# Rows of v by SP transfers split by parity on the DRAM side, and a new order of all steps, in a fused long-convolution and MLP-mixer kernel

## The chip, the cores and the metric

The kernel runs on one core of a Trainium2 chip. The metric is the device time of one execution in microseconds (us). A core has TensorE (PE), VectorE (DVE), ScalarE (ACT), GpSimd (POOL) and SyncE (SP, which only issues transfers), each with an instruction stream of its own that runs in order, and 16 DMA engines that move data between the DRAM and the on-chip memory (SBUF, 128 partitions). PE writes its sums to PSUM, from where DVE and ACT take them.

## The reference

Two blocks work on the same x = A_q (2048 rows of 640 numbers, bfloat16) and a gate mixes them. The inputs A_k and A_v have the same shape; B_x is not used.

```python
k_shift = sum over t in 0..3 of k shifted down by 3-t rows, times shift_k[:, 3-t]   # short causal convolution
kv = k_shift * v
y  = irfft(rfft(kv, 4096) * rfft(ssm_k, 4096))[:2048] + kv * ssm_D      # long causal convolution
a  = q * y
h  = gelu(layernorm(x) @ w1)            # w1 640 x 640
hs = (four groups of 160 columns of h, shifted by +1, -1, +2, -2 rows) @ w2
x1 = x + hs
b  = x1 + gelu(layernorm(x1) @ w3) @ w4     # w3 640 x 1536, w4 1536 x 640
g  = sigmoid((x * gate_w).sum(-1))
out = g * a + (1 - g) * b
```

## The kernel before

Partition p holds the 16 rows 16p to 16p+15 of x, k and v; a "tile" t1 (0 to 15) is one such row of every partition, and four tiles make a chunk c. A transfer of one chunk moves, for each of the 128 partitions, 4 × 640 numbers that lie side by side in DRAM (5120 B), 640 KB in all. The row views `q_rows`, `k_rows`, `v_rows` (L63) have this form.

**v and its rows.** The transform of kv works on even and odd p apart, so the tile KV (R1) holds v with even p in partitions 0 to 63 and odd p in 64 to 127. `v_load(c)` (L571) fills chunk c through `take` (L172): an indirect transfer, issued by POOL (L174), which takes for each partition the DRAM row named in ROWS. `row_order` (L218) writes ROWS by two iota instructions. Four such gathers load v.

**kv.** `k_load(c)` brings k (L560) and transposes it on PE with the same parity (KT). `tap(q)` works on one half of the tiles (q // 5: 1 is tiles 8 to 15, which need v2 and v3; 0 is tiles 0 to 7, with v0 and v1) and one group of 128 columns (q % 5): PE makes the four-tap convolution of k by small matmuls (L590); then either ACT copies it out of PSUM (L598) and DVE multiplies it into KV in place (L601), or DVE multiplies from PSUM (L604).

**Long convolution.** A transform in steps: `step1` on PE (KV at L424, the kernels of ssm_k at L422, loaded by `load_h`, L187), copies out of PSUM by ACT (L369) or DVE (L371), a round trip through DRAM (S_x, S_h; sent at L434, gathered at L441), `step2` (L462), `product` (DVE), `step3` (L509, sent at L520 to S_g), `gin` (L534, back from S_g), and `step4` (PE L875), whose result is multiplied by q and the gate, by ACT (L879) and DVE (L882) or by DVE alone (L885), and added to the sum in X. Its q comes by `load_q(c)` (L858), a transfer on SP, one for each chunk.

**MLP.** `load_x` (L190, L193), `x_stats(c)` (row statistics: DVE bn_stats L684 or two ACT passes with a row sum, L678 and L680), `x_norm` (L661, L663), `x_turn` (transposed by PE, or by a transfer, L651), `mlp1(c, u)` (W1, loaded at L196; PE L709, gelu on ACT L712; its sums lie in the two PSUM banks `psm`), row shifts, `w2` (weights L206 and L207: the first transfer brings four groups of 128 rows, the second the last 32 rows of each group, 4 × 32 rows onto 128 partitions; PE L786), `x1_norm`, `w3` (PE L834, gelu L839), `w4` (PE L852, DVE L854), `store` (L845). Small single-row transfers are ssm_D's (L405) and Zs (L728).

**Order.** `ORDER` (L893 on) is one list for the whole kernel, such as `v_load.3:0`: the step name, its arguments and which piece of it. Each engine runs its instructions in the order in which this list emits them; nothing reorders them later. Letters in a name say which engine evicts (A for ACT, V for DVE). `SLOTS` (L66) says for each allocation of a tag which of its buffers it takes: tag c is four PSUM banks, m the two psm banks, row, gt, xt, gq, ax, hp are SBUF rings. An allocation waits until the users before it in that buffer are done.

SP issues nearly all transfers, in one queue, and its first ones are, in order: x0 (two halves), k3, k1, k2, shift_k, x1, k0, W1, x3, W2 (two), x2, h3, h0, gate_w. POOL issues v3, v2, v0, v1 beside them.

Of the kernel before, what the change touches and what calls it, by code (L numbers as in the profile page):

```python
# [16 lines left out]
P = 128  # L17
S = 2048
D = 640
F = 1536  # L20
NT = 16
# [20 lines left out]
def kernel(  # L42
# [17 lines left out]
    V, A, G, PE, SP = nc.vector, nc.scalar, nc.gpsimd, nc.tensor, nc.sync  # L60
# [6 lines left out]
        "c": "012310320123102130120132013021320321010231302301203120321302103120302130213023012301203102310230"  # L67
             "123013201230312312010132013013012031023302131203012213020132030210312031023301230213102321003212"
             "130120310230132103210232031130220313120132002132013201323100231103232010123302130213021302130132"
             "0012301230123013213",  # L70
        "m": "01010101010101010101010101010101010101010101010101010101010101010101",
        "row": "01230132013120023102130213012030213030301",
        "gt": "012312002103120123012301201",
        "xt": "010101",
        "gq": "01210212012021012012101210110120120",
        "ax": "0123021302310312",
        "hp": "01231302",
# [91 lines left out]
    def by_row():  # L169
        return bass.IndirectOffsetOnAxis(ap=ROWS[:], axis=0)  # L170

    def take(dst, rows, t):  # L172

        G.indirect_dma_start(out=dst, out_offset=None, in_=rows, in_offset=by_row(), element_offset=t * D)  # L174
# [686 lines left out]
    def step4(t1, ev):  # L861
# [240 lines left out]
```

## Time and profile before

| | us |
|---|---|
| median of 3 runs (238.97 to 239.47) | 239.30 |
| the profiled execution | 239.24 |
| its span, first to last instruction | 237.5 |
| PE busy | 224.6 |
| DVE busy | 194.7 |
| ACT busy | 174.0 |
| POOL busy | 16.9 |

The profile tells of one execution. The span is shorter than the execution by what lies before the first and after the last instruction. Busy time of an engine is the sum of its instructions; a row such as `PE 8986...` gives the busy share, in tenths, in each of 40 equal slices of the span (some 5.9 us each). In the lists of instructions a row has the start, the busy time, the engine, the line of the kernel, the operation, what is written and read, and how many of them stand in the row; in brackets, how long the engine was idle before it and what released it. For a transfer the trace also keeps landing records: one time stamp for each DMA engine whose share has landed, up to 16 for a transfer (some records are missing). v's four gathers landed at 17.72 to 19.85 (v3), 19.82 to 21.98 (v2), 28.67 to 30.11 (v0) and 30.33 to 32.70 us (v1); x2 landed at 23.62 to 26.94.

### The profile page before, as it was taken

What the parts mean: (1) busy time and instruction counts of PE and PEld (TensorE: products, weight loads), DVE (VectorE), ACT (ScalarE), POOL (GpSimd) and SP (SyncE); (2) the same over time, 40 slices, a digit from 0 to 9 for tenths busy, and PEclk for the clock granted to TensorE, in tenths of its full rate; (3) what the DMA queues carried; (4) which work ended last, traced back from release to release, by engine and by line L of the source; (5) the groups of instructions that cost most, each with busy time, mean ns of one, the idle gap of its engine ahead of it and who ended that gap; (6) DMA issues with size and microseconds to landing.
All of it is one profiled execution on the core that took longest, in us unless ns stands there. A gap on an engine that the chain in (4) does not pass through costs nothing.

```text
span 237.5 us, 5627 instructions
## 1 busy us (share of the span) xinstructions
PE 224.6 (95%) x2241; PEld 115.8 (49%) x2260; DVE 194.7 (82%) x458; ACT 174.0 (73%) x311; POOL 16.9 (7%) x34
## 2 busy tenths in 40 slices
PE   8986999999999999999999999999999999999791
PEld 3764655533755555444544343444444445456551
DVE  7996999998998999875798897686895988129793
ACT  4796999878887989999697887673698533547560
POOL 4415022000000200021200000000000000000000
PEclk9999999999999999999999999999999999999999
DMA  6999919761999699996899902499950456399672
GB/s 248 375 391 353 359 60 197 182 246 56 382 354 294 212 361 208 353 385 261 286 278 190 354 1 89 130 272 317 360 163 5 139 196 198 138 272 369 190 276 110
DMA packets 42743, 57.06 MB, mean 240 GB/s; under 512 B 20313, under 2 KB 35418, under 8 KB 42462
## 3 DMA queue, kind: packets, MB, share of 16 engines
q1 hardware_dynamic: 42142, 54.10, 71.3%
q0 software_dynamic: 576, 2.62, 2.8%
q8 instruction: 17, 0.28, 0.5%
q14 instruction: 8, 0.07, 0.1%
HBM read 34.42 MB, written 18.36 MB: 222 GB/s over the span
## 4 chain that ended last, share of the span: by engine, by line
PE 87%; DMA 5%; DVE 3%; issue 2%; ACT 1%; SPq 0%; ACTq 0%
PE ps L834 22%; PE ps L852 20%; PE psm L709 10%; PE psw L786 9%; PE ps L462 5%; DMA WA<-in_B_w_dram 5%; PE ps L875 4%; PE ps L422 4%; PE psk L590 3%; PE ps L509 3%; PE psz L227 3%; PE ps L424 3%; PE pst L395 2%; PE pst L618 1%; DVE X L854 1%
## 5 line engine op out<-in xcount | busy, mean ns | idle before, releaser
L852 PE MATMUL ps<-W,gt 128*128 128x128 bf16 (+1 forms) x370 | 54.7, 296 | 1.2 <-issue 0.8
L834 PE MATMUL ps<-x1t,W 128*128 128x512 bf16 x240 | 55.6, 380 | 0.0
L852 PEld LDWEIGHTS <-gt 128*128 128x128 bf16 x384 | 29.0, 98 | 25.2 <-issue 4.9
L834 PEld LDWEIGHTS <-W 128*128 128x128 bf16 x240 | 21.9, 98 | 28.5 <-issue 4.7
L369 ACT CAST gs<-ps 128x320 bf16<-128x320 f32 x40 | 14.9, 433 | 20.4 <-PE ps L509 14.0
L369 ACT CAST stg<-ps 128x512 bf16<-128x512 f32 x46 | 24.8, 594 | 6.7 <-PE ps L424 3.7
L839 ACT ACTIVATE gt<-ps 128x1024 bf16<-128x1024 f32 x24 | 24.7, 1036 | 3.9 <-PE ps L834 3.8
L709 PE MATMUL psm<-xt,WA 128*128 128x512 bf16 x100 | 23.5, 380 | 1.8 <-DMA WA<-in_B_w_dram 1.8
L371 DVE CAST stg<-ps 128x512 bf16<-128x512 f32 x34 | 22.5, 684 | 2.1 <-PE ps L422 1.3
L786 PE MATMUL psw<-WA,HT 128*128 128x128 bf16 (+1 forms) x112 | 21.1, 296 | 0.4 <-issue 0.2
L879 ACT ACTIVATE y<-ps,GS 128x320 bf16<-128x320 f32 x23 | 11.5, 527 | 8.7 <-PE ps L875 6.4
L369 ACT CAST hs<-ps 128x512 bf16<-128x512 f32 x25 | 13.6, 598 | 3.4 <-PE ps L462 3.4
L371 DVE CAST XS<-ps 128x512 bf16<-128x512 f32 x17 | 11.3, 685 | 5.6 <-PE ps L462 5.6
L369 ACT CAST XS<-ps 128x512 bf16<-128x512 f32 x23 | 12.6, 595 | 4.2 <-PE ps L462 4.1
L709 PEld LDWEIGHTS <-WA 128*128 128x128 bf16 x100 | 9.0, 98 | 13.3 <-DMA WA<-in_B_w_dram 2.0
L371 DVE CAST hs<-ps 128x512 bf16<-128x512 f32 x15 | 10.1, 688 | 6.6 <-PE ps L462 6.5
L371 DVE CAST gs<-ps 128x320 bf16<-128x320 f32 x24 | 11.1, 486 | 5.2 <-PE ps L509 4.7
L786 PEld LDWEIGHTS <-HT 128*128 128x128 bf16 x116 | 10.0, 98 | 10.5 <-issue 0.8
L854 DVE SCALAR_TENSOR_TENSOR X<-ps,OMG,X 128x640 bf16<-128x640 f32 x16 | 14.0, 877 | 0.6 <-PE ps L852 0.6
L462 PE MATMUL ps<-ax,CMP 64*32 64x512 bf16 (+3 forms) x512 | 12.9, 300 | 0.1
L885 DVE SCALAR_TENSOR_TENSOR q<-ps,GS,q 128x320 bf16<-128x320 f32 x9 | 4.8, 546 | 10.0 <-PE ps L875 10.0
L788 DVE SCALAR_TENSOR_TENSOR X<-psw,X 128x640 bf16<-128x640 f32 x16 | 12.9, 818 | 0.2
(150 smaller groups left out, 362.6 us busy)
## 6 DMA issues: line engine op xcount, KB each, us to landing
S_x<-stg SPq DMA_DIRECT2D x8, 640.0 KB
S_h<-stg SPq DMA_DIRECT2D x8, 640.0 KB
ax<-S_x SPq DMA_DIRECT2D x8, 640.0 KB
ax<-S_h SPq DMA_DIRECT2D x8, 640.0 KB
S_g<-gs SPq DMA_DIRECT2D x8, 640.0 KB
W<-in_B_w_dram SPq DMA_DIRECT2D x2, 1920.0 KB
kn<-in_A_k_dram SPq DMA_DIRECT2D x4, 640.0 KB
q<-in_A_q_dram SPq DMA_DIRECT2D x4, 640.0 KB
```

Of the source, the lines that this page charges most:

```text
L369: A.copy(out=dst, in_=src)
L371: V.tensor_copy(out=dst, in_=src)
L422: PE.matmul(ps[r][:], lhsT=F1N[:, r].rearrange("p a b -> p (a b)"), rhs=src[:, o + 512 * u:o + 512 * u + 512], start=True, stop=True)
L462: PE.matmul(ps[j][q:q + 32, lo - 512 * u:hi - 512 * u], lhsT=CMP[HALF[j], 8 * b + 4 * h + i, c, :], rhs=st[name, 2 * b + h][HALF[j], i, lo ...
L709: PE.matmul(ps[:, v, :].rearrange("p (a b) -> p a b", a=4), lhsT=W1N[:, k, 160 * f:160 * f + P] if f < 4 else W1M[:, k, :], rhs=xt[:, :, k ...
L786: PE.matmul(ps[:, o:o + w], lhsT=h_tile(f, t1), rhs=W2P[:, f, o:o + w], start=(f == 0), stop=(f == 4))
L788: V.scalar_tensor_tensor(out=X1[:, t1, :], in0=ps[:], scalar=1.0, in1=X[:, t1, :], op0=ALU.mult, op1=ALU.add, accum_out=S12[:, 0, t1:t1 + 1])
L834: PE.matmul(ps[:, u, :].rearrange("p (a b) -> p a b", a=4), lhsT=st["W3"][:, k, f * P:(f + 1) * P], rhs=xt[:, :, k, :], start=(k == 0), st ...
L839: A.activation(out=gt[:, 2 * (fp % 2):2 * (fp % 2) + 2, :], in_=ps[:], func=ACT.Gelu_apprx_tanh)
L852: PE.matmul(ps[:, o:o + w], lhsT=st["gt", c, f // 4][:, f % 4, i * P:(i + 1) * P], rhs=st["W4"][:, f, o:o + w], start=(f == 0), stop=(f == ...
L854: V.scalar_tensor_tensor(out=X1[:, t1, :], in0=ps[:], scalar=OMG[:, t1:t1 + 1], in1=X1[:, t1, :], op0=ALU.mult, op1=ALU.add)
L879: A.activation(out=box["y"][:], in_=box["ps"][:], func=ACT.Copy, scale=GS[:, t1:t1 + 1])
```

## The change

`take` no longer gathers by indices on POOL. It issues on SP a plain transfer whose DRAM side is written out by hand: two groups (even p, odd p), 64 rows in each, 4 × 640 numbers in a row. The SBUF side is the 128 partitions as before. The bytes and the size of a packet stay.

```diff
 def take(dst, rows, t):
-    G.indirect_dma_start(out=dst, out_offset=None, in_=rows, in_offset=by_row(), element_offset=t * D)
+    SP.dma_start(out=dst, in_=bass.AP(tensor=rows.tensor, offset=rows.offset + t * D, ap=[[NT * D, 2], [2 * NT * D, P // 2], [1, 4 * D]]))
```

In the built program the DRAM side has the outer sizes 2, 64 and the SBUF side 128.

`ORDER` is written anew from beginning to end, and with it the strings of `SLOTS` for c, row, gt, gq, ax and hp and some of the letters that choose the evicting engine. The parts that the prediction speaks of:

```diff
-        "open.L1.left:0 open.A2.right:0 warm:0 load_x0.0:0 consts0:0 warm:1 kv_alloc:0 pow0:0 warm:2 load_x0.1:0 "
-        "consts0:1 f1_table:0 k_load.3.AAA:0 row_order:0 f1n_table:0 x_stats.0.VVVA:0 k_load.1.VAA:0 warm:3 f1n_table:1 "
...
+        "k_load.0.AVV:0 k_load.1.AAA:1 x_stats.0.VVVA:5 k_load.3.AAA:4 load_w1:0 v_load.3:0 k_load.1.AAA:4 kv_consts:0 "
+        "k_load.2.AAV:1 k_load.1.AAA:2 x_stats.0.VVVA:6 k_load.1.AAA:6 k_load.2.AAV:3 x_norm.0.VVVV:0 v_load.2:0 "
+        "x_norm.0.VVVV:1 x_norm.0.VVVV:2 k_load.2.AAV:5 k_load.2.AAV:2 k_load.2.AAV:4 x_norm.0.VVVV:3 load_x.3:0 "
+        "k_load.2.AAV:6 x_turn.0.VAV:0 x_turn.0.VAV:1 x_turn.0.VAV:4 v_load.0:0 x_turn.0.VAV:2 x_turn.0.VAV:3 "
+        "x_turn.0.VAV:5 v_load.1:0 f1n_table:1 x_stats.1.VVVV:0 tap.7.AA:0 tap.7.AA:1 tap.9.VA:0 load_h.2:0 tap.7.AA:3 "
...
+        "tap.6.VA:0 tap.6.VA:1 load_x.2:0 tap.5.AV:2 load_w2:0 x_stats.3.VVAA:1 k_load.0.AVV:3 tap.8.VA:3 "
...
+        "x_norm.3.VVVV:3 mlp1.1.1:0 tap.3.AA:1 tap.4.AV:4 x_turn.3.D:0 step1.KV.3.VAAAAVAAAA:0 x_stats.2.VVAA:0 "
```

SP's first transfers are then, in order: x0 (two halves), k3, k1, shift_k, k2, x1, k0, W1, v3, v2, x3, v0, v1, h2, x2, W2 (two), gate_w, h1, h3. `row_order` stands late, where nothing uses what it writes. At the end of the kernel `load_q.1` and `load_q.2` stand just before `gin.0.1` and `gin.0.2`; before, `load_q.2` stood behind `gin.1.1`, after six more gin transfers, and `load_q.1` well ahead of the first gin. ACT loads its function tables five times where it did so six times. PE's 2260 matmuls are the same, and from the middle of the long convolution on nearly in the same order.

More of the change, by code (lines that the diff above doesn't have):

```diff
@@ L66 @@
     SLOTS = {
[L67 to L70, printed above, removed]
+        "c": "012310230212312031231201320132013023131201032120312032013031203120310213201320310123120321031023"
+             "120301230120321031223132013201203210123301230212301012313201302132032103102132032103102132020131"
+             "320123030210312312013202301201331023210231032103102103201233210102321033210213003123012301231203"
+             "1023102301203210212",
         "m": "01010101010101010101010101010101010101010101010101010101010101010101",
-        "row": "01230132013120023102130213012030213030301",
-        "gt": "012312002103120123012301201",
+        "row": "01230120312103032130210231320132021021021",
+        "gt": "012301212312323012301201301",
         "xt": "010101",
-        "gq": "01210212012021012012101210110120120",
-        "ax": "0123021302310312",
-        "hp": "01231302",
+        "gq": "01220221012120120121012021021201201",
+        "ax": "0123031203210312",
+        "hp": "01230312",
     }
```

297 rows, old and new, of the table ORDER are left out of this document.

## The prediction

> **What bounds the kernel now.** I read the page's busy shares first, then its 40 slices, then the table of waits, then the windows and the timeline of 10 to 45 us and of the end.
>
> ```profile
> span 237.5 us, 5627 instructions
> PE 224.6 (95%) x2241; PEld 115.8 (49%) x2260; DVE 194.7 (82%) x458; ACT 174.0 (73%) x311; POOL 16.9 (7%) x34
> PE   8986999999999999999999999999999999999791
> POOL 4415022000000200021200000000000000000000
> DMA  6999919761999699996899902499950456399672
> ```
>
> TensorE is busy 224.6 of 237.5 us; only the start and the last three slices have room. POOL, whose queue issues the four gathers of v, is busy 7%: it is no bound, and freeing it buys nothing by itself. The DMA row shows 9s at the start: there the 16 DMA engines are full.
>
> ```profile
> PE psm L709 <- DMA WA<-in_B_w_dram: 1.8, 1, 1.8
> DVE KV L604 <- DMA KV<-in_A_v_dram,ROWS: 1.8, 1, 1.8
> PE ps L875 <- DVE q L885: 1.2, 1, 1.2
> ```
>
> The columns are total us, times, longest. PE waits 1.8 us for W1 at 20.05, DVE 1.8 us for v at 22.08, and PE 1.2 us at 221.61 for DVE L885, which itself waited until 221.01 for the q rows of `load_q.2` (landed 218.55 to 220.92).
>
> ```profile
> 15.00:20.00 5.00, 3.16 (x56) 2.53 (x54) 4.83 (x20) 4.98 (x10) 0.30 (x1) 1.00 1.02 398
> 30.00:35.00 5.00, 5.00 (x60) 2.85 (x60) 4.63 (x18) 5.00 (x11) 1.34 (x2) 1.00 0.17 55
> 35.00:40.00 5.00, 5.00 (x60) 2.82 (x61) 4.86 (x17) 4.88 (x11) 0.76 (x1) 1.00 0.94 130
> ```
>
> Columns: window, length, busy us of PE, PEld, DVE, ACT, POOL (instructions), granted clock, DMA share, GB/s. In 15 to 20 us DMA is full and ACT and DVE are saturated, so an earlier W1 alone could give little. From 30 us on PE has no gap, and it has none up to the end stage: **whatever delays PE at 40 us delays the end one for one.**
>
> **Parts of the change, one: how many engines carry a load of v.** A gather of v (640 KB, 128 packets of 5120 B) landed in 1.4 to 2.4 us by its landing records (one for each engine's share: v3 17.72 to 19.85, v0 28.67 to 30.11, 16 records each). The new transfer moves the same 128 packets, but its DRAM side begins with an outer size of 2 and its SBUF side with 128. What does the trace show of transfers whose sides begin with different sizes? Those that begin with 128 (or gin's 64 against 32) leave up to 16 records. The second W2 transfer (L207), which begins with 4 on the DRAM side and 128 on the SBUF side, leaves three (24.58 to 25.63), while L206 beside it leaves 15. The single-row transfers (ssm_D L405, Zs L728) leave two each: one about 0.16 us after the issue ends and before data could be there (L728: 55.28), one when the data has landed (56.01). So a transfer need not use all 16 engines, and the missing shares are reported at once. It is not proof: x1's 128-row load left 7 records, so records get lost. I read it as: the number of engines is what divides both outer sizes, at most 16. For v that is **2 engines**, 64 packets each; the other end is 16.
>
> The Trainium skill, page "DMA: Bandwidth & Descriptors", section "Why a DMA increments its semaphore by 16 and not by 1", states this rule: the largest k up to 16 that divides the slowest dimension (other than 1) of both patterns, and on queues such as SP's the lowest-numbered k engines. By it all four loads go through the same pair of engines. The records of L207 and L728 agree as far as they go; no run here shows which engines they were.
>
> Price: a 5120 B packet takes 196 ns (median of this size; mean 219 with the crowded start). 64 × 0.196 = 12.5 us for a load, against 8 × 0.196 = 1.6 on 16 engines; the k loads, each 1.6 to 2 us behind the last, agree with that.
>
> **Two: the queue behind them.** SP's order is new: x0, x0, k3, k1, shift_k, k2, x1, k0, W1, v3, v2, x3, v0, v1, h2, x2, W2 (two), gw, h1, h3. Each engine serves its shares in this order (landings of one queue follow the issue order in the trace). The pair is free when its share of W1 is done: before, 14 of W1's 16 records fell at 14.91 to 15.41, the last at 20.00 behind gathers; I take 16.0 (15.0 to 17.4). Then
> - v3 at 28.5, v2 at 41.1;
> - x3's share, 8 × 0.196 = 1.6: 42.7;
> - v0 at 55.2, v1 at 67.7;
> - h2's share, 8 packets of 4096 B by 159 ns, 1.3: 69.0;
> - x2's share, 1.6: **70.6**.
>
> The gathers had landed by 32.70, x2 by 26.94.
>
> **Three: who waits.** DVE needs v2 and v3 for taps 5 to 9 and v0 and v1 for taps 0 to 4. It now stops at its first v3 product until 41 and works some 12 us of taps and x3 statistics up to 53. The next, tap 4's product (L604), waits for v1 until 67.7; behind it in DVE's order stand all its statistics of x2, later taps and evictions. ACT stands at its first pass over x2 (L678), and behind that, in its order, are the gelus of `mlp1` chunk 1 (L712) that free the two psm banks; PE stands at `mlp1.1.2` for that bank. All three engines are in order, so nothing overtakes. The rows:
>
> ```profile
> 32.42 0.76 ACT L678 ACTIVATE jk<-X 128x640 bf16<-128x640 bf16 x1
> 32.83 0.69 DVE L604 TENSOR_TENSOR KV<-psk,KV 128x512 bf16<-128x512 f32 x1 [0.27 <-PE psk L590]
> 37.97 1.94 ACT L712 ACTIVATE HT<-psm 128x1024 bf16<-128x1024 f32 x2
> 39.60 1.25 PE L709 MATMUL psm<-xt,WA 128*128 128x512 bf16 x5
> ```
>
> ACT's first x2 pass goes from 32.42 to 70.6, 38.2 us later. PE had the bank at about 39.0 and came to it at 39.60, so 0.6 is slack: **+37.6** on PE. By DVE's way (32.83 to 67.7) it is 34.9, so x2 decides. If ACT does the casts that stood between these rows (2.75 us: L598 1.58, L369 0.59 and 0.58) during its wait, the shift is 34.9 instead; its order has them behind the x2 pass, so I take 37.6.
> The transfers behind x2 (W2, h1, h3) land 2 to 4 us later than it; their users stand at 50 us and more in the old order, some 88 in the new, so they are covered. S_x sends and the h loads come later still.
>
> **Four: PE's clock after a stop.** PE will stand for some 25 us. The first 11 warm-up matmuls come 0.425 us apart, later ones 0.216, though the granted clock reads 1.00 throughout. At most this start is paid again (11 × 0.21 = 2.3), at least nothing; **+1.0**, since behind the stop PE waits on ACT and DVE in places.
>
> **Five: the end.** `load_q.2` (issued at 212.53 behind six gin loads) now comes before `gin.0.1` and `gin.0.2`. The 1.2 us of PE's wait and DVE's go: −1.3. `gin.0.2`, issued at 207.08 and landed at 211.25 with its user at 211.80, comes behind two more transfers: +0.7 (0 to 2). ACT loads its function tables 5 times instead of 6; the one at 130.07 (1.28 us, begun while ACT waited 1.26 for PE): −0.3 (−1.3 to 0). Together **−0.9**.
> The gathers gone from POOL (4 × 1.0 us) and `row_order` moved late: 0, POOL is idle beside them. DVE and ACT exchange some evictions, PE's 2260 matmuls are the same and from 90 us on almost in the same order: 0 (−1 to +1), since PE stays the bound there.
>
> **Sum.** Against the profiled execution, 239.24 us (span 237.5; the median of the runs is 239.30, so nothing is lost between them): 239.24 + 37.6 + 1.0 − 0.9 = 276.9, so **277 us**. Low: start 15.0 (−1.0), no casts in between (−2.7), no cold clock (−1.0), end −1.5 more: 270.7. High: start 17.4 (+1.4), packets at their mean of 219 ns (256 of them on the pair's way, +6), cold +1.3: 285.6. So 270 to 286.
>
> **Rivals.**
> - *All 16 engines carry v* (L207's records are merely lost). Then v lands 1.6 us a piece from about 17 on, without POOL's issues between; W1 is no longer held to 20.00 by gathers. The waits at 20.05 and 22.08 go, but ACT's 4.98 of 5 us in 15 to 20 leaves some 0.5 of it. 239.24 − 0.5 − 0.9 = **237.8** (236 to 238.7), faster. Against it: the early landing records of L728.
> - *Sixteen engines, and the new order costs more than it gives*: `gin.0.2` behind q.2 and `gin.0.1`, 1 MB or 2.6 us of all engines, comes to its user 2 us late, of which 1.3 is not won back, and x2 behind both v0 and v1 is 0.3 late: **240.3**, slower. It decides when `gin.0.2` lands later than 211.8 plus the shift.
> - *Two engines, but another pair for each load*: the four run side by side, each 12.5 us from about 16 on, v3 by 28.5, v0 and v1 by 31 to 33. DVE's first product moves from 22.08 to 28.5, 6.4 us, and x2 is not held. 239.24 + 6.4 − 0.9 = **244.7** (243 to 248). Nothing in the trace tells which engines a transfer takes.
> - *No measurable change*: what the start gives, `gin.0.2` takes.
>
> **Chances.** Same pair (270 to 286) 0.80; sixteen and faster 0.08; own pairs 0.06; sixteen and slower 0.04; no change 0.02. A measurement of this kernel tells about 0.2% (0.5 us) from no change. The forecast's own range holds 8 in 10 by itself. Faster 0.08, same 0.02, slower 0.90.
>
> **What would show it.** In the profile after, v's four loads should land 12 to 13 us behind each other (28, 41, 55, 68), two records each beside the early one; the 40 slices should show PE, DVE and ACT near 0 between about 24 and 70 us and a DMA share near 2/16; the table of waits should name KV <- DMA v for DVE (some 15 + 15 us) and x2 for ACT; PE's wait for L885 at the end should be gone. If v lands within 2 us of its issue, step one is wrong and the first rival holds; if the four land together near 30, the third.

## The result, and the profile after

The changed kernel takes **286.86 us** (285.53 to 288.84), the kernel before 239.24 us (238.97 to 239.47): ratio 1.1998, 95% interval 1.1926 to 1.207. The forecast was 277, 270 to 286: the direction and the two long stops came as predicted, but the time is 10 us above the forecast and just above its range. The profiled execution took 287.11 us.

First the page of the changed kernel, the lines that answer to those of before.

```profile
span 285.3 us, 5618 instructions
PE 232.0 (81%) x2241; PEld 117.8 (41%) x2260; DVE 193.4 (68%) x456; ACT 174.0 (61%) x312; POOL 13.2 (5%) x30
...
PE   8791009800469999999899999999999999999993
...
PEclk9997555965597999999999999999999999999999
DMA  7924111641985428969999499750899305399943
```

There are two holes in PE's row, slices of 7.1 us each: from the fourth slice on, and again at about 57 to 71 us. They were not there before. In the depth of both, DMA is at 1 tenth of its 16 engines, and the clock that PE was granted falls to a half. The table of waits (total us, times, longest) names them:

```profile
DVE KV L604 <- DMA KV<-in_A_v_dram: 37.4, 2, 20.4
PE psk L590 <- DVE KV L604: 20.3, 1, 20.3
ACT jk L678 <- DMA X<-in_A_q_dram: 20.3, 2, 20.0
PE ps L424 <- DVE KV L604: 16.5, 1, 16.5
PE psm L709 <- DMA xt<-xn: 2.4, 1, 2.4
```

The windows (columns as before) put numbers on a hole, and on what follows the second:

```profile
30.00:40.00 10.00, 0.00 (x0) 0.00 (x0) 0.00 (x0) 0.00 (x0) 0.00 (x0) 0.50 0.13 52
60.00:70.00 10.00, 0.00 (x0) 0.00 (x0) 0.00 (x0) 0.00 (x0) 0.00 (x0) 0.50 0.16 60
70.00:80.00 10.00, 4.64 (x12) 1.40 (x11) 5.35 (x18) 5.34 (x12) 0.09 (x1) 0.51 0.92 148
```

No engine computes; DMA moves 52 GB/s at 0.13 of 16 engines, that is two. In the trace's packet records of 30 to 32 us there are 20 packets of 5120 B, in pairs, a pair every 0.196 us, each 0.200 us long: two engines, working without a gap. They are called the pair below.

Each load of v left one landing record 0.4 us behind the end of its issue and two when its data was there: v3 28.79 and 29.77, v2 41.16 and 42.18, v0 56.76 and 58.22, v1 69.79 and 71.64. The transfers of 128 rows queued behind them are cut in the same way: x2 has 14 records at 57.22 to 58.75 and two at 72.64 and 74.50. The second W2 transfer, 4 outer rows, has one early record, two at 69.1 to 69.3 and two at 76.6 to 78.4: four engines, of which two stand in the same line as v. These are the records that before had only hinted at.

### The profile page after: what moved, and what is told of

Read it like the earlier page. It is cut to its first block, busy times and chain, and to the rows that moved or that the text cites. A ratio compares the mean times of both kernels' runs of the same rounds, so it can differ in the third digit from the quotient of the medians.

```text
span 285.3 us, 5618 instructions
## 1 busy us (share of the span) xinstructions
PE 232.0 (81%) x2241; PEld 117.8 (41%) x2260; DVE 193.4 (68%) x456; ACT 174.0 (61%) x312; POOL 13.2 (5%) x30
## 4 chain that ended last, share of the span: by engine, by line
PE 61%; DMA 16%; SPq 16%; ACT 4%; issue 1%; DVE 1%; ACTq 0%
PE ps L852 19%; PE ps L834 17%; DMA X<-in_A_q_dram 8%; SPq L174 7%; PE psw L786 5%; SPq L190 4%; PE psm L709 4%; SPq L187 4%; PE ps L462 4%; DMA xt<-xn 4%; PE ps L875 3%; PE ps L509 2%; DMA kn<-in_A_k_dram 2%; DMA S_h<-stg 2%; PE ps L424 2%; PE pst L395 2%
## 5 line engine op out<-in xcount | busy, mean ns | idle before, releaser
L369 ACT CAST stg<-ps 128x512 bf16<-128x512 f32 x49 | 26.6, 592 | 13.6 <-PE ps L424 7.3
L604 DVE TENSOR_TENSOR KV<-psk,KV 128x512 bf16<-128x512 f32 x8 | 5.4, 682 | 42.5 <-DMA KV<-in_A_v_dram 37.4
L709 PE MATMUL psm<-xt,WA 128*128 128x512 bf16 x100 | 27.0, 419 | 2.4 <-DMA xt<-xn 2.4
L590 PE MATMUL psk<-DG,KT 64*128 64x256 bf16 (+3 forms) x190 | 12.1, 270 | 20.3 <-DVE KV L604 20.3
L371 DVE CAST stg<-ps 128x512 bf16<-128x512 f32 x31 | 20.6, 686 | 5.4 <-PE ps L424 2.4
L424 PE MATMUL ps<-KV,F 64*128 64x512 bf16 x40 | 8.1, 416 | 19.3 <-DVE KV L604 16.5
L598 ACT CAST yk<-psk 128x512 bf16<-128x512 f32 x12 | 6.7, 608 | 21.1 <-DVE KV L601 20.2
L590 PEld LDWEIGHTS <-KT 64*128 64x128 bf16 x190 | 9.3, 105 | 22.9 <-issue 22.0
L371 DVE CAST gs<-ps 128x320 bf16<-128x320 f32 x22 | 10.0, 486 | 9.4 <-PE ps L509 9.3
L678 ACT ACTIVATE jk<-X 128x640 bf16<-128x640 bf16 x5 | 3.7, 738 | 20.4 <-DMA X<-in_A_q_dram 20.3
L371 DVE CAST XS<-ps 128x512 bf16<-128x512 f32 x19 | 12.4, 685 | 5.1 <-PE ps L462 5.1
```

The costliest lines, as they stand in the source:

```text
L369: A.copy(out=dst, in_=src)
L371: V.tensor_copy(out=dst, in_=src)
L424: PE.matmul(ps[r][:], lhsT=F1[HALF[r]].rearrange("p a b -> p (a b)"), rhs=src[HALF[r], o + 512 * u:o + 512 * u + 512], start=True, stop=Tr ...
L590: PE.matmul(ps[e][:, lo:hi, :], lhsT=kt[a], rhs=st["DG"][a, 4 * k + lo - i:4 * k + hi - i, :], start=(i == 0), stop=(i == 7))
L709: PE.matmul(ps[:, v, :].rearrange("p (a b) -> p a b", a=4), lhsT=W1N[:, k, 160 * f:160 * f + P] if f < 4 else W1M[:, k, :], rhs=xt[:, :, k ...
```

## The experiments

**e1: two transfers for each load, one for each parity.** The SBUF side and the DRAM side then both begin with 64.

```diff
-        SP.dma_start(out=dst, in_=bass.AP(tensor=rows.tensor, offset=rows.offset + t * D, ap=[[NT * D, 2], [2 * NT * D, P // 2], [1, 4 * D]]))
+        for r in range(2):
+            SP.dma_start(out=dst[HALF[r]], in_=bass.AP(tensor=rows.tensor, offset=rows.offset + r * NT * D + t * D, ap=[[2 * NT * D, H], [1, 4 * D]]))
```

> The changed kernel with one edit: each load of v is two SP transfers, one for each parity, both sides beginning with 64. Order, bytes and packets stay. Theory A (v ran on two DMA engines, because its outer sizes were 2 and 128): 16 engines carry it now, v lands some 2 to 3 us after the transfer ahead of it, the two stops at 22 to 42 and 60 to 71 us go, 238 to 240.5 us. Rival B (the new order of the steps costs the time): 270 us or more. Rival C (issuing on SP is the cost, whatever the form): SP's issues still take 12 us each, 260 us or more.

Measured 246.32 us, 1.0289 (1.0232 to 1.0346). Sixteen landing records for each transfer of v, and the two stops gone: 40.5 of the 47.6 us go with the outer size of 2, with order and queue unchanged. B and C fall. But A's own number was missed by 6 us: DVE waits 3.4 us for v, and PE 2.7 us for the transposed x3. The 5120 B packets between 16 and 30 us have a median of 366 ns, where the gathers of e3 have 201.

**e2 and e3: the form without the order, and the order without the form.** e2 is the kernel before with the SP transfer in `take`; e3 is the changed kernel with the gather in it and `row_order:0` at the start.

> The kernel before with one edit: the four gathers replaced by the SP transfer with the outer size 2; order as before. Theory A: the four loads take 12.5 us each on one pair of engines, v1 lands after 67 us, x2 and W2 behind or between them, 278 to 295 us. Rival B (the order): 238 to 242 us.

> The changed kernel with the gathers put back on POOL (and the two iotas of row_order at the start, where the gathers need them); the new order otherwise. Theory A: v lands in 2 to 3 us a piece, no stops, 237.5 to 242 us. Rival B (the order): 270 us or more.

e2: 284.75 us, 1.1884 (1.1814 to 1.1953). v3 landed by 30.83, v2 43.59, v0 60.89, v1 75.06, x2 76.64. e3: 238.98 us, 0.9966 (0.9928 to 1.0004), not to be told from before. The form of the transfer is the cause; the order is neither needed for the loss nor a loss by itself. From e2's table of waits:

```profile
DVE KV L604 <- DMA KV<-in_A_v_dram: 43.9, 2, 23.9
ACT jk L678 <- DMA X<-in_A_q_dram: 21.1, 1, 21.1
```

The same two waits, under the old order.

**e4: the transposing transfer of x3 out of the queue.**

```diff
-load_w2:0 load_gw:0 load_h.1:0 load_h.3:0 x_turn.3.D:0
+x_turn.3.D:0 load_w2:0 load_gw:0 load_h.1:0 load_h.3:0
```

(These are the steps of SP; those between them in the list stay.)

> The changed kernel with the transposing transfer of x chunk 3 issued before both W2 transfers, gate_w and two loads of ssm_k instead of behind them. Theory D (PE's 2.4 us wait for it at 85.78, and 4.1 us of added shift, come from SP's queue): the step of the shift between PE's mlp1.1.2 and mlp1.3.2 goes from 4.1 to under 1, 283 us. Rival E (ACT and DVE are as late as the transfer): 286 to 287 us.

282.26 us, 1.1789 (1.172 to 1.1859), against 1.1998 for the changed kernel. Its table of waits has no line for PE and xt any more. The shift of PE against the changed kernel goes from −1.9 to −6.0 between `mlp1.1.2` and the next matmuls of KV: the 4.1 us that were asked for. D holds, E falls.

**e5: is it the half of the partitions?** In the kernel before, x1 to x3 come in two transfers of 64 partitions each.

```diff
-        SP.dma_start(out=flat(X[:, 4 * c:4 * c + 4, :]), in_=q_rows[:, 4 * c * D:4 * c * D + 4 * D])
+        for r in range(2):
+            SP.dma_start(out=flat(X[HALF[r], 4 * c:4 * c + 4, :]), in_=q_rows[HALF[r], 4 * c * D:4 * c * D + 4 * D])
```

> The kernel before with one edit: x1, x2 and x3 come as two transfers of 64 partitions each (rows side by side, no parity). It asks why the two transfers for each load of v in e1 had packets of 350 to 460 ns instead of 200. Theory H (a transfer that fills only 64 of the 128 partitions is slow): the 5120 B packets of x1 to x3 take 350 ns or more, 240 to 243 us. Rival I (v's rows of one parity, 40 KB apart in DRAM, are slow): packets stay at 196 to 210 ns, 239 to 240 us.

246.67 us, 1.0287 (1.0235 to 1.0339). From 10 to 12 us, while x1's halves came, 5120 B packets took 365 ns (median; 200 before). The window of e5, and the same of before:

```profile
10.00:12.00 2.00, 1.63 (x29) 1.46 (x27) 2.00 (x6) 2.00 (x4) 1.69 (x2) 1.00 1.00 215
```

```profile
10.00:12.00 2.00, 1.88 (x31) 1.67 (x29) 1.69 (x5) 2.00 (x4) 1.68 (x2) 1.00 1.02 384
```

DMA is full in both (1.00, 1.02) and moves 215 GB/s in place of 384. H holds for the packets and I falls: no parity and no wide row distance is in play here. The price was underrated again (240 to 243 expected): in its profile PE waits 6.3 us for W1 and DVE 6.0 us in all for v.

**e6: the two halves from two queues.** Even rows from SP, odd rows from POOL by plain transfers, otherwise e1.

```diff
-        for r in range(2):
-            SP.dma_start(
+        for r, q in ((0, SP), (1, G)):
+            q.dma_start(
...
```

> The changed kernel with each load of v as two plain transfers, even rows from SP's queue and odd rows from POOL's. Theory H: both halves of the partitions are written at the same time, packets of 200 to 270 ns, no long stops, 237.5 to 241 us. Rival I: packets stay at 350 ns or more, 244 us or more.

250.59 us, 1.0427 (1.0355 to 1.0498); packets at 389 ns (median, 16 to 30 us), 217 GB/s from 18 to 20 us. My expectation failed: two queues don't bring the two halves together. The Trainium skill, page "SBUF — State Buffer", section "Can I just issue two DMAs to hit both halves?", says that they do not: all transfers share the same engines, and only one transfer over all 128 partitions reaches all ports. The number here agrees; why the packets of two queues do not mix was not tried.

**e7: two loads of four.** v3 and v2 by gathers, v0 and v1 in the new form; `row_order:0` stands at the start.

```diff
+        if t >= 8:
+            G.indirect_dma_start(out=dst, out_offset=None, in_=rows, in_offset=by_row(), element_offset=t * D)
+        else:
             SP.dma_start(out=dst, in_=bass.AP(...))
```

> The changed kernel with v3 and v2 gathered on POOL (row_order at the start) and only v0 and v1 in the new form on SP. Theory A with one pair for all: from about 18.5 us on the pair takes 12.8 us for each of the two, v1 at 44 to 46, x2 behind it at 47 to 49; the first stop (22 to 42) is gone, one is left of some 14 us, then 0 to 4 us of queue: 255 to 260 us. Rival F (each load has engines of its own, the chain is something else): v0 and v1 together near 32, 246 us or less.

263.1 us, 1.098 (1.0908 to 1.1051). v0 landed at 34.87, v1 at 48.82, x2 at 51.67; one stop, not two:

```profile
48.94 0.69 DVE L607 TENSOR_TENSOR KV<-psk,KV 128x512 bf16<-128x512 f32 x1 [14.92 <-DMA KV<-in_A_v_dram]
51.75 0.74 ACT L681 ACTIVATE jk<-X 128x640 bf16<-128x640 bf16 x1 [17.90 <-DMA X<-in_A_q_dram]
```

Half the loads, half the loss (24 us of 48). A chain through one pair holds, F falls. It came 3 us over its range: v0 to v1 took 14.0 us, not 12.8, and x3's transpose was late again (PE waited 1.8).

**e8, e9 and e12: the 2 us of the new order.** PE's shift (the start of a matmul in a run, less that of the same matmul before) grows by 1.8 to 2.5 us between its second `w2` part and the second transform step in the changed kernel (2.5 at that step's first matmul, 2.3 behind it), e1 (2.1) and e3 (1.8), and by nothing in e2. This growth is called the step here. In e3 (and so without the stops) a copy waits there for a send of S_h to leave its buffer:

```profile
ACT stg L369 <- DMA S_h<-stg: 2.4, 1, 2.4
```

e8 moves two gathers of S_x behind sends of S_h (pieces 15 and 16 of `step1.HT0`), e9 the x1 transpose (`x1_norm.0`, piece 6, L813), e12 both, all from e3. SP's steps alone, first e8, then e9, then e12:

```diff
-gather.x.0:0 step1.HT0.2.AAAAAVAVAV:16 gather.x.7:0 step1.HT0.3.AAAVVAAAAA:16 x1_norm.0.VVVA:6 step1.HT0.3.AAAVVAAAAA:15
+step1.HT0.2.AAAAAVAVAV:16 gather.x.0:0 step1.HT0.3.AAAVVAAAAA:16 gather.x.7:0 x1_norm.0.VVVA:6 step1.HT0.3.AAAVVAAAAA:15
...
+gather.x.0:0 step1.HT0.2.AAAAAVAVAV:16 gather.x.7:0 step1.HT0.3.AAAVVAAAAA:16 step1.HT0.3.AAAVVAAAAA:15 x1_norm.0.VVVA:6
...
+step1.HT0.2.AAAAAVAVAV:16 gather.x.0:0 step1.HT0.3.AAAVVAAAAA:16 step1.HT0.3.AAAVVAAAAA:15 x1_norm.0.VVVA:6 gather.x.7:0
```

> The kernel of e3 (new order, gathers of v) with two transfers moved: the first two gathers of S_x stand behind the sends of S_h that they passed. In the changed kernel, in e1 and in e3 PE lost 2.1 to 2.3 us between its w2 part and the second transform step, in e2 (old order) 0. Theory G (the sends of S_h wait behind those gathers, and the copies into their buffers wait for them): that step shrinks to under 0.7, 237 us. Rival J (something else of the new order): the step stays, 238.5 to 239 us.

> The kernel of e3 (new order, gathers of v) with one transfer moved: the transposing transfer of the first normed x1 chunk (L813, 4.8 us of SP's time in e3) stands behind the send of S_h that it kept waiting, not ahead of it. Theory K (that send, and so the copies into its buffer, is what costs the new order 2.1 us at 82 to 102 us): the step shrinks to under 0.8 and the time is 236 to 238 us. Rival J (the step has another source, or the transposed chunk is then late by as much): 238.5 us or more.

> The kernel of e3 with the moves of e8 and e9 together: the two sends of S_h go ahead of both the first two gathers of S_x and the x1 transpose (order: sends, one gather, sends, transpose, gather, much as in the kernel before). Each move alone left the step of 2.1 to 2.8 us at 82 to 102 us. Theory N (the DMA queue ahead of these sends is the cause, and each move alone left one of the two transfers in it): the step falls under 0.8, 236.5 to 238 us. Rival J (the step comes from the order of the copies and matmuls themselves): it stays over 1.8, 239 us or more, and stays open.

e8 241.56 us, 1.0078 (1.0043 to 1.0113), the step 2.75; e9 240.86 us, 1.0067 (1.0017 to 1.0116), the step 2.2: theories G and K each fell. e12: **238.07 us, 0.9956 (0.9924 to 0.9988)**, where 236.5 to 238 was expected, the step 0.5, and of ACT's wait for S_h 0.2 us is left, where it was 2.4 in e3 and e8 and 2.8 in e9. By the profiles, one of each kernel, N holds: the sends were behind both, and either one alone was enough to make the copy late. In e3 the x1 transpose kept SP from 85.03 to 89.81, and the next send of S_h was issued at 89.86. In time the gain is not shown: e12 (0.9956) can't be told from e3 (0.9966), and e8 and e9 lie 1% above e3, more than their steps explain. e12 is 0.4% under the kernel before, and no run shows that the new order is worth more.

**e10: the same form from POOL's queue.**

```diff
-        SP.dma_start(out=dst, in_=bass.AP(...))
+        G.dma_start(out=dst, in_=bass.AP(...))
```

> The changed kernel with v's four transfers, in the same form (outer sizes 2 and 128), issued by POOL instead of SP. Each is still 64 packets of 200 ns on one engine, 12.8 us at least. Theory L (POOL's queue also uses the same pair of engines each time, so the four follow each other): v1 after 65 us, 265 us or more; x2 and the other loads are no longer kept by SP's issue. Rival M (POOL's queue takes another pair for each load, as the Trainium skill states in 'DMA: Bandwidth & Descriptors', section 'Why a DMA increments its semaphore by 16 and not by 1'): the four run side by side, the last of them lands by 30 to 36 us, some 7 to 10 us of stop, 245 to 250 us.

266.35 us, 1.1037 (1.0969 to 1.1106); its profile is of the longest of its four executions, 271.36 us. The time fits L (265 us or more), but not L's chain. By the landing records the loads do run side by side on different pairs: all 16 shares are reported when their engines come to them, and the number that is late grows by two from load to load, 2 for v3, 4 for v2, 6 for v0, 8 for v1. That is M's mechanism, without M's time: v3, issued at 2.84, landed at 41.83, and v2, v0 and v1, issued at 11.7 to 14.2, at 54.5, 58.9 and 61.6; packets of 5120 B took a mean of 497 ns between 16 and 37 us, and k2, x1, k0 and W1 had shares on these engines too, late with them (PE waited 20.5 us for k2). Why packets are that long there is open.

**e11: x2 ahead of v0 and v1.**

```diff
-v_load.0:0 v_load.1:0 load_h.2:0 load_x.2:0
+load_x.2:0 v_load.0:0 v_load.1:0 load_h.2:0
```

> The changed kernel with the load of x2 issued before v0 and v1 instead of behind them. Step under test: the second stop ends with x2 (landed 74.5, ACT at 74.58), not with v1 (71.64). If so x2 is there by 46 us, v1 and the first product of tap 4 come 1.6 us later than now, at 73.3, and PE goes on 1 to 2.5 us earlier than now behind it: 284 to 286 us (changed kernel 286.9). If v1 was as late as x2 for what PE waits for: 287 to 289 us.

285.91 us, 1.1952 (1.1898 to 1.2007), against 1.1998; the intervals overlap, so the time alone does not show a gain. In its profile x2 was there by 45, v1's product started at 73.19 and PE came to `mlp1.1.2` at 80.94, in the changed kernel at 82.17. In these profiles x2 does decide the end of the second stop: PE is 1.2 us ahead at `mlp1.1.2` and 1.8 at the matmuls of KV behind it. With x2 out of the way, v1 decides.

## Why the forecast held in kind and failed in size

The forecast summed PE's shift to 37.7; it is 47.8 at the end (285.3 − 237.5). The step that failed most is the sentence that the transfers behind x2 are covered: 4.1 us, put at nothing. Besides, x2 was forecast 3.9 us too early (4.0 by ACT's pass over it), and the middle, put at 0, cost 2.3.

| step of the forecast | forecast | measured |
|---|---|---|
| ACT's first pass over x2, from 32.42 to | 70.6 (+38.2) | 74.58 (+42.2) |
| slack of 0.6 used, colder clock +1.0 | +0.4 | +0.4 |
| transfers behind x2, "covered" | 0 | +4.1 |
| the middle (80 to 102 us before), order | 0 (−1 to +1) | +2.3 |
| the end | −0.9 | −1.2 |
| sum | +37.7 | +47.8 |

The rows behind it, timeline of the changed kernel (start, busy us):

```profile
42.27 0.69 DVE L604 TENSOR_TENSOR KV<-psk,KV 128x512 bf16<-128x512 f32 x1 [20.39 <-DMA KV<-in_A_v_dram]
71.77 0.69 DVE L604 TENSOR_TENSOR KV<-psk,KV 128x512 bf16<-128x512 f32 x1 [17.01 <-DMA KV<-in_A_v_dram]
72.51 0.58 PE L424 MATMUL ps<-KV,F 64*128 64x512 bf16 x1 [16.46 <-DVE KV L604]
74.58 0.74 ACT L678 ACTIVATE jk<-X 128x640 bf16<-128x640 bf16 x1 [20.00 <-DMA X<-in_A_q_dram]
75.32 0.57 ACT L598 CAST yk<-psk 128x512 bf16<-128x512 f32 x1
75.94 0.58 PE L424 MATMUL ps<-KV,F 64*128 64x512 bf16 x1 [2.85 <-ACT yk L598]
76.45 3.92 PE L709 MATMUL psm<-xt,WA 128*128 128x512 bf16 x10
80.41 1.02 ACT L712 ACTIVATE HT<-psm 128x1024 bf16<-128x1024 f32 x1 [0.48 <-PE psm L709]
82.17 1.25 PE L709 MATMUL psm<-xt,WA 128*128 128x512 bf16 x5
85.78 1.62 PE L709 MATMUL psm<-xt,WA 128*128 128x512 bf16 x5 [2.35 <-DMA xt<-xn]
```

The ten matmuls of 76.45 stand in the kernel before at 35.46:

```profile
35.46 2.33 PE L709 MATMUL psm<-xt,WA 128*128 128x512 bf16 x10
```

- **Two engines, one pair, a line behind it**: right. The rivals with 16 engines and with a pair for each load are out on SP's queue.
- **The line's times**: 3.9 us too early at x2. The line began later: W1's last two shares landed at 16.92 and 17.80, where 16.0 was taken, and v3 came 1.3 later than forecast (29.77 for 28.5). The price of a packet was right: the pair sent one every 0.196 us, and v2 and x3 took 12.4 and 1.8 us. But v0 took 14.2 and v1 13.4 in place of 12.5. The other 14 engines had h2, x2 and W2 while these ran, and between 52 and 60 us packets of this size, on all engines, took a mean of 224 to 396 ns (in windows of 2 us); v2 ran while the others had nothing. That this is why v0 and v1 took longer is read from the times, not tested. The mean of 219 ns was in the text, for the upper end only.
- **The path behind the stop, and the clock**: the sum of +0.4 came out, its two terms did not, so that is luck. PE did not stand at `mlp1.1.2` for a psm bank. It stood at a matmul of KV (L424), 16.46 us for v1's product and then 2.85 us for ACT's cast L598, which comes behind the first pass over x2. From 75.94 on it had work, and it came to `mlp1.1.2` at 82.17 without a wait; the gelu that frees the bank had ended at 81.43. The pass over x2 is 42.2 us later than before, the ten matmuls 41.0 (76.45 for 35.46), so 1.2 us of slack went in place of 0.6. The ten took 3.92 us for 2.33, at a granted clock of 0.59 (76.4 to 80.4 us; 1.00 before), so the clock cost 1.6 in place of 1.0.
- **What failed most** is the sentence that the transfers behind x2 are covered. It looked at the users of W2, h1 and h3, which landed 2 to 7.5 us behind x2 (forecast 2 to 4) and which no line of the table of waits names. It left out the next transfer in SP's order, the transpose of x3 (`x_turn.3.D`), whose user stands right behind `mlp1.1.2`:

```profile
54.09 11.49 SPq L207 DMA_DIRECT2D WA<-in_B_w_dram  x1
65.62 5.69 SPq L199 DMA_DIRECT2D GW<-in_gate_w_dram  x1
71.36 1.83 SPq L187 DMA_DIRECT2D E<-in_A_ssm_k_dram  x1
73.24 0.43 SPq L187 DMA_DIRECT2D HN<-in_A_ssm_k_dram  x1
73.79 8.38 SPq L651 DMA_TRANSPOSE xt<-xn  x1
```

  Its issue could not begin before 73.79, and it lasted 8.38 us, to 82.17; the transfers ahead of it had their last shares on the pair, the last of them (h3) landing at 82.03. The 14 profiles hold 84 transposing transfers. None ended its issue before everything issued ahead of it on SP had landed, and the nine that found nothing under way took 2.5 to 3.7 us. By these times this one paid for the whole line behind the pair. PE had `mlp1.1.2` done by 83.4 and stood until 85.78, and behind that wait the granted clock was down again (0.59 from 85.8 to 89.8 us). e4, which moves the five transfers behind it, takes 4.1 us away.
- **The middle at 0 (−1 to +1)** was wrong by 2.3, through the order of SP's transfers around the sends of S_h (e12). PE's order was compared there, SP's was not.
- **The end** came out (−1.2 for −0.9), and PE's wait for L885 is gone. But e2, with the old order, also gains 1.1 there, and 0.4 us of that wait is left in it. That the moved `load_q.2` brought the gain is not shown.

## What to carry to other kernels

Before a transfer is rewritten, write down the outer sizes of both its sides: on this queue the number of engines was their common divisor, at most 16 (2 against 128 gave two engines, 4 against 128 four, 64 against 64 sixteen), and a leading size of 2 turned a load of some 2 us into one of 12 to 14. Then list every transfer behind it in the same queue, to the last one that something waits for, since each of them has shares on the slow engines; a forecast that stops at the first late one is too small. Look for a transposing transfer among them, since its issue waited here for all that went before. And two half-height transfers are no repair: rows that must be split by parity over all 128 partitions were cheapest here as a gather, of the forms tried, at some 2 us a load, issued by an engine that was idle.

## What the runs showed of the hardware

- A transfer whose sides begin with 2 and 128 ran on two engines at 52 GB/s, where all 16 moved 398 (15 to 20 us, before), and on SP's queue always on the same two: the four loads landed one behind the other, and two of the four engines of the second W2 transfer were late in the same line. By the Trainium skill ("DMA: Bandwidth & Descriptors", "Why a DMA increments its semaphore by 16 and not by 1") these are the lowest-numbered, and POOL's queue takes others in turn; the records of e10 agree with the second.
- Not expected: SP itself stands while the pair is behind. The issue of x3 lasted 12.7 us and that of h2 12.3:

```profile
12.26 12.74 SPq L190 DMA_DIRECT2D X<-in_A_q_dram  x1
25.05 14.79 SPq L174 DMA_DIRECT2D KV<-in_A_v_dram  x2
39.89 12.31 SPq L187 DMA_DIRECT2D E<-in_A_ssm_k_dram  x1
```

  Meanwhile the other 14 engines had nothing (DMA share 0.13), and x2, a transfer they could have begun, was not issued until 52.24. In e2 it is W2's turn (12.97 us). What ends such an issue the trace does not say; it was not tested by itself.
- A transposing transfer on SP kept its issue open until all transfers issued ahead of it had landed: 8.38 us in the changed kernel (82.17, the last landing at 82.03), 19.58 in e4 (73.02 and 72.81), 8.21 in e7 (59.27 and 59.13), and 2.5 to 3.7 us in the nine of 84 that found nothing under way. Why it waits was not tested.
- Transfers to 64 of the 128 partitions move about half as much with all engines busy: 215 GB/s for 384 (e5), 366 ns a packet for 201 (e1 against e3).
- The granted clock reads 0.50 in a stop of 20 us and 0.51 in the window of 70 to 80 us, in which PE has begun again.
